# Opening loads reordered and tied to TensorE's progress, and one scores visit moved

## The chip, the cores and the metric

The kernel runs on one core of one Trainium2 chip. The metric is the device time of one execution in microseconds (us). Loads from HBM are issued on two hardware queues here: most by the SyncE sequencer (SP), a few at the very start by ScalarE (ACT).

## The reference

```
scores = scale * q @ k.T          # 8 batches, 8 heads, 576 positions, head 64
scores = where(mask, scores, -1e9)  # heads 0-3: the last 32 positions; heads 4-7: 32 of the last 128, every 4th
attn   = exp(scores - max); attn = attn / (sum(attn) + 1e-9)
x      = (attn @ v) laid out as (4608 tokens, 512)
h      = x @ w_in                 # 512 -> 2048
g      = max(h, 0) + log1p(exp(-abs(h)))
out    = g @ w_out                # 2048 -> 512
```

## The kernel before

The 4608 tokens are cut into nine chunks of 512. Attention goes by groups: chunk c and pair of heads, `groups[4c + pr]`. The steps of a group have one letter each. S is the scores (`score`, 64 small matmuls into `s_ps`; the first two chunks add the mask with two more matmuls of a bf16 identity, held in the tile `opened`), M the maximum on VectorE (DVE), E eight exponentials on ACT (line 421), Z the divisor, Pv the division on DVE, T four transposes on TensorE (`t_ps`, line 450), C or Cv the copy back (`pt`), V the product with v (64 small matmuls into `a_ps`), Xh and Xl the split of the result into a high and a low part (`xh`, `xl`). The feed-forward part runs in slots: one slot is one chunk and one of 16 slices ff of the hidden width. `H` is a quarter of the first product (three matmuls 128x512 into `h_ps`), A its three activations on ACT, G the softplus on DVE, Gs and Gl the split into `gh` and `gl`, `O` a quarter of the second product (`o_ps`).

The weights arrive as 64-bit floats. `fetch` loads raw piece r_n as two loads of 256 KB; `decode_step` turns it into two fp32 parts by D0 (ACT) , D1 to D4 (DVE), D5 (ACT) and Dl (DVE). D0_ff_i begins piece (ff, i), i = 0 for w_in and 1 for w_out; r0 is (0, 0), r1 (1, 0), r2 (0, 1), r3 (2, 0).

The first 45 us and some more are written out by hand: the string `OPENING` (line 73) lists the steps, and a loop after line 762 issues them in that order. Each engine works through its own instructions in the order of the string, so a token's place decides only what stands ahead of it on its engine. `F` is a run of filler matmuls on a zeroed tile (`unread`), `r k q v m` are loads. Group loads: k 272 or 320 KB, q 256 KB, v twice 256 KB, the mask of chunk 1 (m1) 128 KB; m0 is the identity and the mask of chunk 0, 160 KB into `opened`. The keys of groups 0 to 2 and m0 go out on ACT's queue, all other loads on SP's. `load_dma` (line 137) lets each of the first THIN = 64 loads on SP wait until the load DEPTH = 8 places earlier has landed. TensorE needs q and k of a group for S, v for V.

After the opening the attention of the later chunks is put between the slots by due times. `attend(n, when, lag)` places, for the groups n and n+1, the scores at slot time `when` (`scores`), the row maxima, exponentials and divisions after it, and the product with v at `when + lag`. A cost given with each step also tells the planner in `tick` when DVE has room for the remaining decoding and for the sums of weights that the later chunks need (`early`). From chunk 2 on the first product is done by sums and differences of blocks (`h_x`, `h_y`).

Of the kernel before, what the change touches and what calls it, by code (L numbers as in the profile page):

```python
# [40 lines left out]
NPR = H // 2  # L41
# [4 lines left out]
FIRST = 2  # L46
# [3 lines left out]
EARLY = 5  # L50
NEG = -1.0e9
DEPTH = 8
THIN = 64
LAG = 2
EXP_AND_LN = [t.name for t in act_sets.SETS].index("natural_log_exp_and_others")

# [14 lines left out]


OPENING = """
F1 r0 k0 m0 q0 r1 k1 q1 r2 k2 q2 k3 q3 v0 q4 k4 m1 v1 r3 k5 v2 q5 v3 r4 r5 D0_0_0 v4 F6 D1_0_0 S0
D2_0_0 D3_0_0 D4_0_0 F1 D5_0_0 D0_1_0 M0 E0 Dl0_0 r6 r7 D1_1_0 D2_1_0 D3_1_0 S1 v5 M1 Z0 D0_0_1 Pv0
D1_0_1 S2 D2_0_1 M2 D3_0_1 E1 Z1 T0 S3 D4_0_1 Pv1 C0 V0 E2 M3 T1 Cv1 Xh0 Xl0 F3 S4 D4_1_0 E3 Z2 M4
q7 Pv2 k7 V1 H0_0 Xh1 D0_2_0 Xl1 D1_2_0 r8 r9 T2 E4 k6 Cv2 Z3 H0_1 D2_2_0 D5_1_0 Pv3 q6 r10 D3_2_0
V2 Dl1_0 S5 M5 D5_0_1 Xh2 Xl2 T3 Dl0_1 H1_0 H1_1 Z4 C3 E5 Pv4 D4_2_0 V3 Z5 Xh3 D0_3_0 D5_2_0 Xl3 Pv5
T4 H0_2 D1_3_0 D2_3_0 H0_3 D3_3_0 C4 V4 A0 H1_2 H1_3 D0_1_1 Xh4 Dl2_0 G0 D1_1_1 H2_0 H2_1 Xl4 H2_2
T5 D2_1_1 D3_1_1 Gs0 Gl0 D0_4_0 A1 D4_3_0 D4_1_1 C5 H2_3 D1_4_0 D2_4_0 G1 O0_0 O0_1 O0_2 O0_3 V5  # L80
D5_3_0 Dl3_0 H3_0 H3_1 H3_2 D5_1_1 D3_4_0 Gs1 H3_3 D4_4_0 Dl1_1 Gl1 O1_0 v7 D0_2_1 D1_2_1 D2_2_1 Xh5
D3_2_1 Xl5 A2 G2 D5_4_0 D4_2_1 r11 Dl4_0 v6 r12 r13 A3 G3 Gs2 D5_2_1 Gl2 D0_5_0 O1_1 r14 Dl2_1 r15
D0_3_1 O1_2 S7 M7 H4_0 H4_1 O1_3 r16 H4_2 D1_5_0 E7 D2_5_0 D3_5_0 O2_0 O2_1 r17 O2_2 H4_3 D4_5_0
D5_5_0 D1_3_1 r18 r19 r20 S6 r21 O2_3 D2_3_1 D3_3_1 r22 Dl5_0 H5_0 H5_1 H5_2 Gs3 A4 M6 Gl3 G4 E6
D4_3_1 Z7 H5_3 Gh4 Pv7 D5_3_1 Dl3_1 H6_0 H6_1 T7 D0_4_1 r23 C7 D1_4_1 Z6 O3_0 O3_1 D2_4_1 A5 Pv6
D3_4_1 D4_4_1 G5 V7 Xh7 Xl7 O3_2 D5_4_1 Dl4_1 Gl4 O3_3 H7_0 T6 D0_5_1 r24 r25 Cv6 H7_1 O4_0 D1_5_1
V6 D2_5_1 D3_5_1 D0_6_0 r26 O4_1 O4_2 O4_3 Gs5 Gl5 Xh6 Xl6 H6_2 H6_3 D1_6_0 D0_6_1 H7_2 D4_5_1
D1_6_1 D2_6_1 D5_5_1 Dl5_1 r27 r28 r29 D3_6_1 A6 D4_6_1 G6 Gh6 Gl6 H7_3 A7 G7 O5_0 O5_1 O5_2 O5_3
H8_0 H9_0 H8_1 r30 r31 K0 D5_6_1 K1 D2_6_0 D0_9_0 D1_9_0 Gs7 H8_2 H8_3 A8 Dl6_1 O6_0 Gl7 H9_1 D3_6_0
D4_6_0 H9_2 H9_3 K2 K3 D5_6_0 D2_9_0 O6_1 D3_9_0 D4_9_0 D5_9_0 G8 Dl9_0 Dl6_0 O6_2 O6_3 Gh8 O7_0 Gl8  # L90
O7_1 O7_2 A9 O7_3 G9 Gh9 Gl9
"""


# [1 line left out]
def tile_windowed_attention_softplus_ffn(  # L96
# [11 lines left out]
    nc = tc.nc  # L108
# [11 lines left out]
    slots, at = [], {0: 0, 1: 0}  # L120
# [11 lines left out]

        tc.keep_in_program_order(ins)

    under_way = []

    def load_dma(engine=None, **kw):
        ins = tc.keep_in_program_order((engine or nc.sync).dma_start(**kw))
        if engine is None and len(under_way) < THIN:
            if len(under_way) >= DEPTH:  # L140
                tc.add_manual_dep(
                    ins.ins,
                    under_way[-DEPTH].ins.name,
                    mybir.DependencyInfo(mybir.DependencyClass.Sync, mybir.DependencyReason.DATA),
                    reason="at most so many of the first loads under way",
                )
            under_way.append(ins)

    def load_halves(out, in_):

        n = out.shape[1] // 2
        for half in (slice(0, n), slice(n, 2 * n)):
            load_dma(out=out[:, half], in_=in_[:, half])

    def fetch(upto):
        for _, ff, i in needed[len(raws) : upto]:
            raw = const.tile([P, DM], mybir.dt.int64, name="raw", tag=f"w{ff}_{i}")
            load_halves(raw, w[ff, :, i * DM : (i + 1) * DM])
            raws[ff, i] = raw
# [40 lines left out]
            wt[ff, i] = parts  # L200

    def matmul(**kw):
        tc.keep_in_program_order(nc.tensor.matmul(**kw))  # L203

    def bank(name, tag):
        return psum.tile([P, CH], F32, name=name, tag=tag, bufs=2 if tag == "h" else 1)
# [31 lines left out]
    def load_mask(c):  # L238
        if c == 0:
            load_dma(nc.scalar, out=consts, in_=cst[0])  # L240
            nc.gpsimd.tensor_copy(out=ident, in_=identb)
            masks[0] = consts[:, P:]
            return
        masks[c] = wk.tile([P, 2 * SW], BF16, name="mask", bufs=2)
        load_dma(out=masks[c], in_=cst[c, :, P:] if c < FIRST else msk[c])
# [75 lines left out]
    class Group:  # L321
# [33 lines left out]
        def score(self, both=None):  # L355

            self.base = 0 if both is None else self.pr % 2 * SW
            self.banks, self.scored = both or two_banks(
                "s_ps", "hh" if self.own and self.pr % 2 else None
            )  # L360
            for t in range(NS):
                for g in range(NG):
                    for r in range(2):
                        rows = slice(r * D, (r + 1) * D)
                        q0, k0 = first_of(self.dil, t, g, self.c >= FIRST)
                        matmul(
                            out=self.banks[r][
                                g * BLK : (g + 1) * BLK,
                                self.base + t * WKEYS : self.base + (t + 1) * WKEYS,
                            ],  # L370
                            lhsT=self.q[rows, q0 : q0 + BLK],
                            rhs=self.k[rows, k0 : k0 + WKEYS],
                            start=not self.masked or t == 0,
                            stop=not self.masked,
                        )
# [214 lines left out]
    groups = [Group(c, pr) for c in range(NCH) for pr in range(NPR)]  # L590
# [38 lines left out]
    def at(when, part, *what, cost=0.0):  # L629
        heapq.heappush(events, (when, next(serial), cost, part, what))  # L630
# [126 lines left out]
    def fillers(n):  # L757
# [3 lines left out]

    parts = {
        "F": fillers,
        "k": lambda g: groups[g].load_k(nc.scalar if g < 3 else None),
        "q": lambda g: groups[g].load_q(),
        "v": lambda g: groups[g].load_v(),
        "m": load_mask,
        "r": lambda n: fetch(n + 1),
        "S": lambda g: groups[g].score(),
        "M": lambda g: groups[g].maximum(),  # L770
# [142 lines left out]
    def attend(n, when, lag, wait=0.0):  # L913

        at(when, scores, n, cost=-1.45)
        for e in range(2):
            g, then = groups[n + e], when + e
            late = 0 if e else wait
            at(then + 0.12 + late, g.maximum, cost=1.34)
            at(then + 0.37 + late, g.exponentials)  # L920
            at(then + 1.0, g.divisor, cost=0.36)
            at(then + 1.0, g.divide)
            at(then + 1.37, turn, n + e, cost=0.65)
            at(then + 1.5, send, n + e)
            at(then + 2.2, bring, n + e)
        at(when + 2.8, load_v, n + 1)
        at(when + 3.45, load_queries, n + 2)
        at(when + lag, values, n, cost=-1.45)
        for e in range(2):
            at(when + lag + 0.25 + 0.25 * e, groups[n + e].turn_rows, cost=0.65)  # L930
        at(when + lag + 0.7, groups[n].send_x)
        back = 3.0 if n == (FIRST + 1) * NPR else 1.25
        at(when + lag + back, groups[n].bring_x)
        at(when + lag + 0.01, load_keys, n + 2)
        at(when + lag + back + 0.05, load_v, n + 2)
# [24 lines left out]
    for ff in range(NFF):  # L960
        at(18 + 0.55 * ff if ff < 4 else 22.4 + 0.4 * (ff - 4), keep_w_out, ff)
    for j in range(2):
        attend(FIRST * NPR + 2 * j, 10.2 + 7.5 * j, 4.125)
    attend((FIRST + 1) * NPR, 26.7, 4.6, 0.25)
    at(26.2, ob_tiles, 0, True)
    for n in range(4):
# [81 lines left out]
    behind = 0.0  # L1048
# [122 lines left out]
    for n, (c, p) in enumerate((c, p) for c in range(FIRST, NCH) for p in range(NPAIR)):  # L1171
        u = 2 * n
        for k, (x, weights, b, first, to, temp) in enumerate(steps):
# [20 lines left out]
    for half in range(2):  # L1194
        ob = const.tile([P, NKT, HALF], F32, name="pt", tag=("s", "v")[half])
        for m in range(NKT):
# [7 lines left out]
            if half and m > 1:  # L1204
                engine = nc.sync if m % 2 else nc.scalar
# [126 lines left out]
```

## Time and profile before

| | |
|---|---|
| median of three timed runs | 867.06 us (866.37 to 868.7) |
| the profiled execution, device time | 867.87 us |
| its span, first to last instruction | 866.0 us |
| TensorE matmul busy | 847.8 us, 98% of the span, 9143 matmuls |
| VectorE, ScalarE busy | 618.3 us, 533.4 us |
| mean granted TensorE clock | 0.996 of full |
| largest shares of the chain that ended last | o_ps 44%, h_x 19%, h_y 14%, h_ps 9% |

The span is read from the first instruction to the last; the device time is 1.87 us longer. TensorE executes its instructions in order, so each idle stretch of it is a row of the timeline with the time and, in brackets, the idle time before it and what ended it. "issue" there means that the engine waited for nothing that the profile shows. The DMA queues are listed by kind: q1 and q10 are the loads and stores that SP and ACT issue, q8 and q14 are of the kind "instruction".

### The profile page before, as it was taken

The page shows a single profiled execution, that of the slowest core. Times are in us where ns is not written, and L with a number is a line of the kernel's source. Part 1 is how long each engine was busy: PE and PEld are TensorE (multiplying, and loading weights), DVE is VectorE, ACT ScalarE, POOL GpSimd, SP SyncE. Part 2 cuts the span into 40 slices and gives each one's busy share as a digit, 9 for nine tenths or more (in the row PEclk, how much of TensorE's full clock was granted, in tenths as well). Part 3 has the DMA queues.
Part 4 walks back from the last instruction along what each step waited for, and adds up shares of the span by engine and source line. Part 5 has one row for each costly group of instructions (what it writes and reads, how often), then busy time and mean ns, then how long its engine had stood idle before and what let it go on. Part 6 is the DMA issues. An engine that isn't in the chain of part 4 may idle for free.

```text
span 866.0 us, 22770 instructions
## 1 busy us (share of the span) xinstructions
PE 847.8 (98%) x9143; PEld 735.5 (85%) x9143; DVE 618.3 (71%) x1260; ACT 533.4 (62%) x1327; POOL 31.4 (4%) x34
## 2 busy tenths in 40 slices
PE   6799999999999999999999999999999999999998
PEld 4478888888888988888888989898889898899997
DVE  5698898898888887576856777576748675665554
ACT  5587778767565767466564665565736564465443
POOL 0000000101000000000000000000000000000000
PEclk9899999999999999999999999999999999999999
DMA  9849445684666475657575656556664754424223
GB/s 329 310 135 383 175 128 172 200 307 167 192 221 207 151 247 179 211 181 231 197 229 158 210 196 218 196 181 216 210 215 154 231 195 157 146 98 146 98 107 113
DMA packets 107305, 168.81 MB, mean 195 GB/s; under 512 B 11072, under 2 KB 41920, under 8 KB 107200
## 3 DMA queue, kind: packets, MB, share of 16 engines
q1 hardware_dynamic: 106480, 166.18, 58.0%
q8 instruction: 72, 1.18, 0.6%
q10 hardware_dynamic: 720, 1.18, 0.4%
q14 instruction: 33, 0.27, 0.1%
HBM read 132.71 MB, written 34.60 MB: 193 GB/s over the span
## 4 chain that ended last, share of the span: by engine, by line
PE 93%; DVE 3%; ACT 2%; issue 1%; DMA 1%; SPq 0%; ACTq 0%
PE o_ps L203 44%; PE h_x L203 19%; PE h_y L203 14%; PE h_ps L203 9%; PE s_ps L203 3%; PE a_ps L203 3%; ACT s L421 1%; DMA raw<-w 1%; PE t_ps L450 0%; DVE e L673 0%; DVE t L843 0%; ACT a L171 0%; DVE b L823 0%; DVE ob L746 0%; DVE gl L691 0%
## 5 line engine op out<-in xcount | busy, mean ns | idle before, releaser
L203 PE MATMUL o_ps<-gh,t 128*128 128x512 f32 (+1 forms) x904 | 341.3, 391 | 0.0
L203 PEld LDWEIGHTS o_ps<-gh,t 128*128 128x128 f32 x904 | 169.8, 188 | 21.6
L666 ACT ACTIVATE e<-hs 128x512 f32<-128x512 f32 x112 | 70.0, 625 | 186.7 <-DVE hs L1100 186.6
L203 PE MATMUL o_ps<-gl,t 128*128 128x512 f32 (+1 forms) x452 | 178.4, 395 | 0.0
L685 ACT CAST gh<-e 128x512 fp32r<-128x512 f32 x140 | 86.4, 617 | 64.5 <-DVE e L673 60.0
L691 DVE TENSOR_TENSOR gl<-e,gh 128x512 fp32r<-128x512 f32 x144 | 103.1, 716 | 5.5 <-ACT gh L685 4.7
L203 PEld LDWEIGHTS h_x<-a,parts 128*128 128x128 f32 x672 | 94.7, 189 | 10.2 <-DVE temps L1098 0.7
L203 PEld LDWEIGHTS h_y<-s,t 128*128 128x128 f32 x672 | 94.4, 188 | 10.0 <-DVE temps L1100 0.2
L203 PE MATMUL h_x<-a,parts 128*128 128x256 f32 x672 | 98.6, 282 | 0.2 <-DVE temps L1098 0.2
L203 PE MATMUL h_y<-s,t 128*128 128x256 f32 x672 | 98.8, 282 | 0.0
L668 ACT ACTIVATE e<-e 128x512 f32<-128x512 f32 x144 | 91.2, 633 | 4.6
L667 ACT ACTIVATE e<-e 128x512 f32<-128x512 f32 x144 | 91.1, 633 | 4.6
L203 PEld LDWEIGHTS o_ps<-gl,t 128*128 128x128 f32 x452 | 86.4, 191 | 3.0 <-DVE gl L691 0.4
L203 PE MATMUL h_ps<-xh,parts 128*128 128x512 f32 x256 | 88.0, 399 | 0.0
L203 PE MATMUL o_ps<-gh,parts 128*128 128x512 f32 x256 | 87.0, 393 | 0.0
L1100 DVE TENSOR_TENSOR hs<-h_x,temps 128x256 f32<-128x256 f32 x112 | 47.3, 422 | 52.5 <-PE h_x L203 51.9
L421 ACT ACTIVATE s<-s,nm 128x64 f32<-128x64 f32 x224 | 74.8, 335 | 5.6 <-DVE nm L413 5.5
L673 DVE SCALAR_TENSOR_TENSOR e<-hs,e 128x512 f32<-128x512 f32 x112 | 76.2, 681 | 1.8 <-ACT e L668 1.8
L1100 DVE TENSOR_TENSOR temps<-h_y,temps 128x256 f32<-128x256 f32 x112 | 47.2, 421 | 41.4 <-PE h_y L203 40.8
L1098 DVE COPY temps<-h_x 128x256 f32<-128x256 f32 x56 | 23.6, 422 | 56.4 <-PE h_x L203 56.3
L203 PEld LDWEIGHTS h_ps<-xh,parts 128*128 128x128 f32 x256 | 48.6, 190 | 10.6 <-DVE e L673 0.5
L203 PEld LDWEIGHTS o_ps<-gh,parts 128*128 128x128 f32 x256 | 48.1, 188 | 9.9
(82 smaller groups left out, 1189.6 us busy)
## 6 DMA issues: line engine op xcount, KB each, us to landing
t<-w_out SPq DMA_DIRECT2D x224, 256.0 KB, 3.2
raw<-w SPq DMA_DIRECT2D x64, 256.0 KB, 5.6
v<-vp SPq DMA_DIRECT2D x28, 512.0 KB, 4.6
q<-qp SPq DMA_DIRECT2D x36, 256.0 KB, 4.9
w_out<-parts SPq DMA_DIRECT2D x16, 512.0 KB, 6.8
out_t<-ob SPq DMA_DIRECT2D x32, 256.0 KB, 2.9
turned<-sq SPq DMA_DIRECT2D x112, 64.0 KB, 2.6
pt<-turned SPq DMA_DIRECT2D x28, 256.0 KB, 2.8
```

Source lines behind the costliest of these rows:

```text
L203: tc.keep_in_program_order(nc.tensor.matmul(**kw))
L421: pin(nc.scalar.activation(out=self.blocks[:, t], in_=src, func=AF.Exp, bias=self.nm[:, t : t + 1], scale=1.0 / 8.0 if self.masked else 1. ...
L666: pin(nc.scalar.activation(out=e, in_=tiles[i], func=AF.Abs))
L667: pin(nc.scalar.activation(out=e, in_=e, func=AF.Exp, scale=-1.0))
L668: pin(nc.scalar.activation(out=e, in_=e, func=AF.Ln, bias=1.0))
L673: pin(nc.vector.scalar_tensor_tensor(out=e, in0=tiles.pop(i), scalar=0.0, in1=e, op0=ALU.max, op1=ALU.add))
L685: pin((copy or nc.scalar.copy)(out=gh, in_=ready[i]))
L691: pin(nc.vector.tensor_tensor(out=gl, in0=e, in1=gh.bitcast(F32), op=ALU.subtract))
L1098: pin(nc.vector.tensor_copy(out=dst, in_=src))
L1100: pin(nc.vector.tensor_tensor(out=dst, in0=src, in1=temps[:, temp], op=ALU.add))
```

## The change

The string `OPENING` keeps the sequence of every engine but SP and ACT's load queue, and its loads stand in another order and mostly later. A new token W remembers the newest matmul issued through `matmul` (not the transposes of T); the next load on SP that follows in the string gets a wait for that matmul. As SP issues in order, all loads behind it are held too. THIN goes from 64 to 128. The keys of group 2 move from ACT's queue to SP's. The second visit of `attend` (groups 10 and 11) has its scores at 16.575 instead of 17.7 slots; its lag goes from 4.125 to 5.25, so its product with v stays at 21.825.

```diff
-THIN = 64
+THIN = 128
 OPENING = """
-F1 r0 k0 m0 q0 r1 k1 q1 r2 k2 q2 k3 q3 v0 q4 k4 m1 v1 r3 k5 v2 q5 v3 r4 r5 D0_0_0 v4 F6 D1_0_0 S0
+m0 q0 r0 k1 k0 F1 D0_0_0 F6 r1 D1_0_0 S0 q1 D2_0_0 k2 D3_0_0 r2 D4_0_0 F1 D5_0_0 D0_1_0 M0 E0 W1 q2
...
     def load_dma(engine=None, **kw):
         ins = tc.keep_in_program_order((engine or nc.sync).dma_start(**kw))
+        if engine is None and gate:
+            depends(ins, gate.pop(), "loads behind what TensorE does")
...
     def matmul(**kw):
-        tc.keep_in_program_order(nc.tensor.matmul(**kw))
+        newest[:] = [tc.keep_in_program_order(nc.tensor.matmul(**kw))]
...
-        "k": lambda g: groups[g].load_k(nc.scalar if g < 3 else None),
+        "k": lambda g: groups[g].load_k(nc.scalar if g < 2 else None),
...
+        "W": lambda _: gate.append(newest[0]),
...
-        attend(FIRST * NPR + 2 * j, 10.2 + 7.5 * j, 4.125)
+        attend(FIRST * NPR + 2 * j, (10.2, 16.575)[j], (4.125, 5.25)[j])
```

The gated loads and their gates, in SP's order: q2 and q3 behind the filler after S0; k4 (then m1) behind S2; q4 (then v1, r3) behind S3; q5 (then v2, k5, r4, v3) behind S4; q7 (then r5, v4, r6) behind V2; k7 (then r7, r8, v6, v5, r9, k6, r10, r11) behind V3; v7 (then q6, r12, r13 to r16) behind O1_1; r17 to r31 behind three later steps.

First place: SP at the start of the program, before. A DMAHW name is the lane of an earlier load whose landing is awaited.

```order
L138 DMA raw<-w 128x256 x2
L138 DMA q<-qp 128x512
L138 DMA raw<-w 128x256
L138 DMA raw<-w 128x256 [waits DMAHW0_50]
L138 DMA q<-qp 128x512 [waits DMAHW1_50]
L138 DMA raw<-w 128x256 [waits DMAHW2_50]
L138 DMA raw<-w 128x256 [waits DMAHW3_50]
L138 DMA q<-qp 128x512 [waits DMAHW4_50]
L138 DMA k<-kdl 128x640 [waits DMAHW5_50]
L138 DMA q<-qp 128x512 [waits DMAHW6_50]
L138 DMA v<-vp 128x512 [waits DMAHW7_50]
L138 DMA v<-vp 128x512 [waits DMAHW0_50]
```

The same place of SP in the change, from the first load to the first of k4; PE is the wait that W adds.

```order
L146 DMA q<-qp 128x512
L146 DMA raw<-w 128x256 x4
L146 DMA q<-qp 128x512 [waits DMAHW0_50]
L146 DMA k<-kdl 128x640 [waits DMAHW1_50]
L146 DMA raw<-w 128x256 [waits DMAHW2_50]
L146 DMA raw<-w 128x256 [waits DMAHW3_50]
L146 DMA q<-qp 128x512 [waits DMAHW4_50,PE_50]
L146 DMA q<-qp 128x512 [waits DMAHW5_50]
L146 DMA k<-kdl 128x640 [waits DMAHW6_50]
L146 DMA v<-vp 128x512 [waits DMAHW7_50]
L146 DMA v<-vp 128x512 [waits DMAHW0_50]
L146 DMA k<-kpl 128x544 [waits DMAHW1_50,PE_50]
```

q0 stands ahead of r0 and r1 now, the third q (q2) waits for TensorE, and what follows v0 begins with a gated k4.

Second place: ACT at the start of the program, before.

```order
L138 DMA k<-kpl 128x544
L138 DMA opened<-cst 128x640
L138 DMA k<-kpl 128x544
L138 DMA k<-kdl 128x640
L171 ACTIVATE a<-raw 128x512
```

ACT in the change, to the decoding of r1.

```order
L146 DMA opened<-cst 128x640
L146 DMA k<-kpl 128x544 x2
L176 ACTIVATE a<-raw 128x512
L199 CAST parts<-a 128x512
L176 ACTIVATE a<-raw 128x512
```

m0 is first, k1 and k0 follow, and k2 is no longer here; the work behind the loads keeps its sequence.

Third place: TensorE (PE) in slots 16 and 17, in the change, where the scores of groups 10 and 11 stand now.

```order
L208 MATMUL s_ps<-k,q 32x64 x64
L208 MATMUL o_ps_1458<-gh,parts 128x512
L208 MATMUL o_ps_1458<-gl,parts 128x512
L208 MATMUL o_ps_1458<-gh,parts 128x512
L208 MATMUL o_ps_1469<-gh,parts 128x512
L208 MATMUL o_ps_1469<-gl,parts 128x512
L208 MATMUL o_ps_1469<-gh,parts 128x512
```

PE before, one slot later, where the same scores stood.

```order
L203 MATMUL o_ps_1458<-gh,parts 128x512
L203 MATMUL s_ps<-k,q 32x64 x64
L203 MATMUL o_ps_1469<-gh,parts 128x512
L203 MATMUL o_ps_1469<-gl,parts 128x512
L203 MATMUL o_ps_1469<-gh,parts 128x512
```

The visit stands 27 matmuls of 128x512 earlier; nothing else moves on TensorE. On DVE and ACT the row maxima and exponentials of this visit move up by about as much, and some decoding steps and sums of weights move down behind them.

## Rows read from the trace of the kernel before

**Rows 1.** The page's part 1: busy us, share of the span and instructions of each engine.
```profile
PE 847.8 (98%) x9143; PEld 735.5 (85%) x9143; DVE 618.3 (71%) x1260; ACT 533.4 (62%) x1327; POOL 31.4 (4%) x34
```

**Rows 2.** TensorE's waits from 45 us on: engine, line, releaser: us, times, longest.
```profile
PE h_x L203 <- DVE hs L1098: 0.6, 1, 0.6
PE h_x L203 <- DVE temps L1098: 0.2, 1, 0.2
```

**Rows 3.** Timeline of PE, 0 to 44 us: start, us, what [idle before <- releaser].
```profile
8.13 1.17 PE L203 MATMUL s_ps<-k,q 64*32 64x64 f32 x64 [3.43 <-DMA q<-qp]
...
13.40 1.18 PE L203 MATMUL s_ps<-k,q 64*32 64x64 f32 x64 [0.78 <-ACT s L421]
...
17.21 1.10 PE L203 MATMUL s_ps<-k,q 64*32 64x64 f32 x55 [0.40 <-issue]
...
18.79 1.94 PE L203 MATMUL a_ps<-pt,v 64*64 64x32 f32 x64
...
24.09 1.12 PE L203 MATMUL a_ps<-pt,v 64*64 64x32 f32 x60
27.29 0.30 PE L203 MATMUL a_ps<-pt,v 64*64 64x32 f32 x4 [2.07 <-issue]
...
31.00 0.73 PE L203 MATMUL s_ps<-k,q 64*32 64x64 f32 x48 [0.17 <-ACT s L421]
35.75 0.47 PE L203 MATMUL s_ps<-k,q 64*32 64x64 f32 x16 [4.02 <-issue]
...
43.50 1.14 PE L203 MATMUL a_ps<-pt,v 64*64 64x32 f32 x64 [0.31 <-ACT pt L488]
```

**Rows 4.** Windows from one stop of PE to the next: busy (xcount), clock, DMA, GB/s.
```profile
16.90:27.20 10.30, 8.00 (x254) 5.76 (x253) 6.57 (x18) 5.68 (x35) 0.00 (x0) 1.00 1.01 353
27.20:35.70 8.50, 4.18 (x126) 3.22 (x127) 3.91 (x9) 4.88 (x22) 0.00 (x0) 0.85 1.00 334
```

**Rows 5.** The page's part 3, one queue of kind instruction: packets, MB, share.
```profile
q8 instruction: 72, 1.18, 0.6%
```

**Rows 6.** DMA from 24.8 to 33.3 us: packets, queue, issues with us to landing.
```profile
DMA packets 1462, 2.66 MB, mean 313 GB/s; under 512 B 164, under 2 KB 164, under 8 KB 1462
...
q1 hardware_dynamic: 1462, 2.66, 97.3%
...
raw<-w SPq DMA_DIRECT2D x7, 256.0 KB, 6.3
```

**Rows 7.** DMA from 33.3 to 33.6 us: the instruction queue's packet.
```profile
q8 instruction: 1, 0.02, 19.8%
```

**Rows 8.** DMA from 43.8 to 45 us: all packets, and their queue.
```profile
DMA packets 1, 0.02 MB, mean 14 GB/s; under 512 B 0, under 2 KB 0, under 8 KB 0
...
q8 instruction: 1, 0.02, 6.2%
```

**Rows 9.** Timeline of SP's queue around 25 us: start, us, loads issued.
```profile
24.77 3.03 SPq L138 DMA_DIRECT2D raw<-w  x4
```

**Rows 10.** DMA from 53.3 to 53.7 us: a load issued into empty queues.
```profile
v<-vp SPq DMA_DIRECT2D x1, 256.0 KB, 3.1
```

**Rows 11.** Timeline of ACT, 6 to 43 us: start, us, what [idle before <- releaser].
```profile
6.64 0.66 ACT L171 ACTIVATE a<-raw 128x512 f32<-128x512 f32 x1 [4.63 <-DMA raw<-w]
...
10.87 0.31 ACT L421 ACTIVATE s<-s_ps,nm 128x64 f32<-128x64 f32 x1
...
15.90 0.35 ACT L421 ACTIVATE s<-s_ps,nm 128x64 f32<-128x64 f32 x1
...
28.48 0.31 ACT L421 ACTIVATE s<-s_ps,nm 128x64 f32<-128x64 f32 x1
...
41.24 0.65 ACT L584 CAST xh<-a_ps 128x256 fp32r<-128x256 f32 x2 [0.63 <-PE a_ps L203]
```

**Rows 12.** Windows around PE's longest stop: busy of PE, PEld, DVE, ACT, POOL, then clock.
```profile
32.00:36.00 4.00, 0.25 (x16) 0.23 (x15) 0.18 (x1) 0.52 (x2) 0.00 (x0) 0.64 1.02 370
36.00:40.00 4.00, 4.00 (x28) 2.85 (x12) 3.10 (x9) 2.35 (x14) 0.00 (x0) 0.50 1.04 396
```

**Rows 13.** Windows around the old place of the moved scores visit (same columns).
```profile
135.00:145.00 10.00, 10.00 (x166) 8.21 (x165) 9.20 (x18) 8.13 (x15) 0.00 (x0) 1.00 0.25 95
```

More of the change, by code (lines that the diff above doesn't have):

```diff
@@ L73 @@
 OPENING = """
-F1 r0 k0 m0 q0 r1 k1 q1 r2 k2 q2 k3 q3 v0 q4 k4 m1 v1 r3 k5 v2 q5 v3 r4 r5 D0_0_0 v4 F6 D1_0_0 S0
[L75 to L90, printed above, removed]
@@ L91 @@
-O7_1 O7_2 A9 O7_3 G9 Gh9 Gl9
+m0 q0 r0 k1 k0 F1 D0_0_0 F6 r1 D1_0_0 S0 q1 D2_0_0 k2 D3_0_0 r2 D4_0_0 F1 D5_0_0 D0_1_0 M0 E0 W1 q2
+Dl0_0 D1_1_0 D2_1_0 W1 D3_1_0 S1 q3 M1 Z0 D0_0_1 Pv0 D1_0_1 S2 D2_0_1 M2 D3_0_1 E1 k3 Z1 v0 T0 W1 k4
+S3 m1 W1 q4 D4_0_1 v1 r3 Pv1 C0 V0 E2 M3 T1 Cv1 Xh0 Xl0 F3 S4 D4_1_0 E3 Z2 M4 Pv2 W1 W1 V1 H0_0 Xh1
+D0_2_0 Xl1 D1_2_0 T2 E4 q5 Cv2 Z3 v2 k5 H0_1 D2_2_0 r4 D5_1_0 v3 Pv3 D3_2_0 V2 Dl1_0 W1 S5 M5 D5_0_1
+Xh2 Xl2 T3 Dl0_1 H1_0 H1_1 Z4 C3 E5 Pv4 D4_2_0 q7 V3 Z5 Xh3 r5 D0_3_0 v4 r6 D5_2_0 W1 Xl3 Pv5 T4
@@ new lines @@
+H0_2 D1_3_0 k7 D2_3_0 H0_3 D3_3_0 C4 V4 A0 H1_2 H1_3 D0_1_1 Xh4 Dl2_0 r7 r8 v6 G0 D1_1_1 H2_0 H2_1
+Xl4 H2_2 T5 D2_1_1 D3_1_1 Gs0 Gl0 D0_4_0 A1 D4_3_0 D4_1_1 v5 C5 H2_3 r9 D1_4_0 D2_4_0 G1 O0_0 O0_1
+O0_2 O0_3 V5 D5_3_0 Dl3_0 H3_0 H3_1 H3_2 D5_1_1 D3_4_0 Gs1 H3_3 D4_4_0 Dl1_1 Gl1 k6 O1_0 D0_2_1
+D1_2_1 D2_2_1 Xh5 D3_2_1 Xl5 A2 G2 D5_4_0 D4_2_1 Dl4_0 A3 r10 G3 Gs2 D5_2_1 Gl2 D0_5_0 r11 O1_1
+Dl2_1 D0_3_1 W1 O1_2 S7 v7 M7 H4_0 H4_1 O1_3 H4_2 D1_5_0 E7 D2_5_0 D3_5_0 O2_0 O2_1 O2_2 q6 H4_3
+D4_5_0 D5_5_0 D1_3_1 S6 O2_3 D2_3_1 D3_3_1 r12 Dl5_0 H5_0 H5_1 H5_2 Gs3 A4 M6 Gl3 G4 E6 D4_3_1 Z7
@@ new lines @@
+H5_3 Gh4 Pv7 D5_3_1 Dl3_1 H6_0 H6_1 T7 D0_4_1 C7 D1_4_1 r13 Z6 O3_0 O3_1 D2_4_1 A5 Pv6 D3_4_1 D4_4_1
+G5 V7 Xh7 r14 r15 r16 Xl7 O3_2 W1 D5_4_1 r17 r18 r19 r20 Dl4_1 Gl4 O3_3 H7_0 T6 D0_5_1 W1 Cv6 H7_1
+r21 O4_0 D1_5_1 V6 D2_5_1 D3_5_1 D0_6_0 O4_1 O4_2 O4_3 Gs5 r22 r23 r24 Gl5 Xh6 Xl6 H6_2 H6_3 D1_6_0
+r25 r26 r27 r28 r29 D0_6_1 H7_2 D4_5_1 D1_6_1 r30 D2_6_1 D5_5_1 Dl5_1 D3_6_1 W1 A6 D4_6_1 G6 Gh6 Gl6
+H7_3 A7 G7 O5_0 O5_1 O5_2 O5_3 r31 H8_0 W1 H9_0 H8_1 K0 D5_6_1 K1 D2_6_0 D0_9_0 D1_9_0 Gs7 H8_2 H8_3
@@ L92 @@
+A8 W1 Dl6_1 O6_0 Gl7 H9_1 D3_6_0 D4_6_0 H9_2 H9_3 K2 K3 D5_6_0 D2_9_0 O6_1 D3_9_0 D4_9_0 D5_9_0 G8
+Dl9_0 Dl6_0 O6_2 O6_3 Gh8 O7_0 Gl8 O7_1 O7_2 A9 O7_3 G9 Gh9 Gl9
 """
@@ L133, in pin, with depends @@
         tc.keep_in_program_order(ins)
-    under_way = []
+    under_way, gate, newest = [], [], []
+    def depends(ins, on, reason):
+        tc.add_manual_dep(
+            ins.ins,
+            on.ins.name,
+            mybir.DependencyInfo(mybir.DependencyClass.Sync, mybir.DependencyReason.DATA),
+            reason=reason,
+        )
     def load_dma(engine=None, **kw):
         ins = tc.keep_in_program_order((engine or nc.sync).dma_start(**kw))
+        if engine is None and gate:
+            depends(ins, gate.pop(), "loads behind what TensorE does")
         if engine is None and len(under_way) < THIN:
             if len(under_way) >= DEPTH:
[L141 to L146, printed above, removed]
+                depends(ins, under_way[-DEPTH], "at most so many of the first loads under way")
             under_way.append(ins)
```

## The prediction

> **What bounds the kernel now.** I read the page's busy times first: TensorE is busy for 98% of the span [rows 1], so only time that it loses can be won. Its waits from 45 us to the end add up to 0.8 us [rows 2]; the rest of its idle time lies in the first 45 us, which the change rewrites. The timeline of that stretch [rows 3] shows three kinds of loss. S0 waits for q0 until 8.13. S2 waits until 13.40 for ACT, whose exponentials E0 must free the bank. And three times TensorE waits for "issue", that is for nothing that the profile shows: 0.40 us in S3, 2.07 in V1, 4.02 in S5.
>
> What are these three? Between the first and the second stop lie 254 matmuls, between the second and the third 126 [rows 4]. Each matmul has a weight load, so that is about 508 and 252 instructions. The page counts 9143 matmuls and 9143 weight loads [rows 1] and 72 packets on the instruction queue q8 [rows 5]: 18286 / 72 = 254 per packet. So TensorE stops where a block of its own instructions ends and the next is not there. The DMA rows agree: from 24.8 to 33.3 us all 1462 packets belong to q1, none to q8 [rows 6]; TensorE stops at 31.73 (31.00 + 0.73); the q8 packet begins between 33.3 and 33.6 [rows 7]; TensorE goes on at 35.75, some 2.4 us after it.
>
> Why is it late? I read it as queued behind loads. SP issued four raw loads from 24.77 over 3.03 us [rows 9], and loads of that stretch take 6.3 us to land [rows 6]. TensorE entered the last block before the stop at 27.29, and 27.29 + 6.3 = 33.6, just where the packet is. With no load under way, a single packet of q8 passes between 43.8 and 45 us [rows 8], and TensorE doesn't stop for it. [...]
>
> **The change part by part.** THIN, 64 to 128: nothing. In the order, loads beyond the eighth already wait for a lane that an earlier load holds, and the added wait names a load of that kind.
>
> The moved visit: nothing on TensorE's sum, which keeps its 64 matmuls per group. It stands 27 matmuls earlier; TensorE is busy for the whole of its window, and DVE for 9.20 of 10 us [rows 13]. What DVE does later for it is decoding and sums of weights, and TensorE shows no wait for these in that stretch [rows 2]. Bounds: a gain of the 0.8 us of waits there are, a loss of as much. On SP the loads and sends of the visit move up past some stores of w_out, on POOL its divisions move up; neither is waited for there. I take 0.
>
> The first loads: m0, k1 and k0 on ACT's queue, q0, r0 and r1 on SP's. S0 needs q0, k0 and m0. Up to now r0 led: its second half was down when ACT began decoding at 6.64 [rows 11], and S0 got q0 at 8.13. Now q0, m0 and k1 go ahead of r0 and k0 beside it: 256 + 160 + 272 + 512 + 272 = 1472 KB until r0 and k0 are complete. That is what r0, k0, m0, q0 and k1 were, and of those q0 ended the wait at 8.13. So S0 stays near 8.1, and r0 comes at about 8.1 instead of 6.64, **1.5 us later** (bounds 0 and 2). Decoding of r0 stands ahead of M0 on DVE and ahead of E0 on ACT, so E0 moves from 10.87 [rows 11] to 12.4, S2 from 13.40 to 14.9, and the last exponential of E1 from 15.90 + 0.35 = 16.25 to 17.75. S3 needs the bank that E1 frees; its last 55 matmuls now run from 17.21 because of the stop [rows 3]. Without the stop they would run from 17.75: **+0.55** for V0 (18.79 to 19.35). k2, moved to SP behind r1 and q1, is in about 512 + 256 + 320 KB later, at 353 GB/s [rows 4] near 11.2, well before S2. Most of the late start is thus covered by the 0.40 us stop and the time that S3 already lost.
>
> The gates: what is queued when TensorE enters a block. At 353 GB/s [rows 4] a 256 KB load takes 0.74 us of queue. For the stop in V1 the block before begins at the fillers, about 22.6 in the new count. Ahead of its refill stand q4, v1 and r3: five loads, 3.7 us, released by S3's end at 19.5. For the stop in S5 the block before begins at V1's end; the gate on S4 (24.9) lets q5, v2 and k5 out by then, four loads, about 3 us, where eight were under way. A load into empty queues lands in 3.1 us [rows 10], one behind others in 6.3 [rows 6]. So the refills still wait, but behind a queue that was empty shortly before and has been draining since. The bounds of each stop are 0 and what it is today, 2.07 and 4.02. Counting from when data begin to move, about 1 us after issue, I get queue ends near 24 and 28.5, and with 2.4 us to restart, 26.4 and 30.9, against 25.8 and 30.6 wanted. I take **0.7 us left of each**: -1.35 and -3.3.
>
> [...] I take 0.63, and 0.12 on the end of S5: **-0.75**, between 0 and -2.0.
>
> What the gates delay: q4 is wanted at S4, about 23.6. Released at 19.5, it lands at 22.6 by [rows 10]. v2's second half, the third load behind S4, is wanted near 28.5 and lands at 24.9 + 3.1 + 2 x 0.74 = 29.5 by the same count, less if the 3.1 holds the wait of its own refill. That is level, so I add nothing. v6 waits for V4 and holds v5 back, with 7 us until V5. Later pieces have many slots.
>
> Sum: +0.55 - 1.35 - 3.3 - 0.75 = -4.85 us. The profiled execution took 867.87 us, so 863.0. The median of the runs shown is 0.81 lower: 862.2.
>
> **The rivals.** *The refills still queue.* Each gate lets out a burst that stands ahead of the next refill. For it: loads are issued 0.4 us apart once free, and both refills come 2 to 3 us after a gate. Then V1's stop stays at 2.07, S5's goes to 1.9 by the smaller burst, and the clock holds: 0.55 - 2.1 - 0.75 = -2.3, 864.8.
>
> *Everything is covered.* Both stops go, and r0 comes early enough that S3 follows E1 without loss: -2.07 - 4.02 - 0.75 - 0.4 = -7.25, 859.8.
>
> *The stops have nothing to do with the loads.* The packets of q8 would come when they come; only the late r0 remains, and the stops of 2.07 and 4.02 stay: 867.06 + 0.55 = 867.6. Against it stand the 6.3 us that fit and the unharmed refill at 44 us. [...]
>
> *Slower: TensorE starves and stays at the low clock.* The place is S4. If q4 lands more than 4.1 us after its gate, S4 waits; at 6.3 it begins at 25.8, 2.2 us late. The gap could keep the lower level through V2: V0 took 1.94 us there and V4 1.14 at the higher, so V1 and V2 lose 1.6, S4 and S5 0.6, transposes and six h matmuls about 2.0. v2, behind the next gate, would be late by 2.2 again. With the 0.55 that is 0.55 + 2.2 + 2.2 + 4.2 = 9.15, against 6.1 for the stops, which slower work would hide, and nothing from the clock: +3.05, 870.1.
>
> **How the numbers follow.** A measurement of this kernel tells about 0.3%, 2.6 us, from no change. Forecast 0.60; refills still queue 0.14; all covered 0.13; stops unrelated 0.07; starved 0.06. Faster by over 2.6 us: 0.60 + 0.13 + 0.04 of the second case = 0.77. Within: 0.10 + 0.06 = 0.16. Slower: 0.07, the starved case and a little of the unrelated one. The range 859.3 to 865.9 takes in the second and the third case and leaves out the last two.
>
> **What would show it.** Right: "issue" before V1 and S5 under 1 us each; granted clock 1.00 from 24 to 40 us; ACT's first decoding near 8.1; V4 near 38.7 instead of 43.5; no new wait after 45 us. Wrong: a wait for DMA at S4, V2 or S5, an "issue" stop of 2 us or more, or a clock that falls again.

## The result and the profile after

The change made the kernel **slower: 872.17 us** (median of five executions, 870.92 to 875.06) against 867.06 us (865.92 to 868.89), a ratio of 1.0056 with the interval [1.0039, 1.0073]. Forecast were 862.2 us and a range of 859.3 to 865.9. The profiled execution has a span of 872.7 us, 6.7 us more than before; its device time, 875.06 us, is the longest of the five, so it shows somewhat more than the 5.1 us between the medians. The page's part 1, after (engine, busy us, share of the span, instructions), answers to [rows 1]: TensorE is busy 5.2 us longer with the same matmuls (one record fewer), and idle 1.5 us longer (19.7 against 18.2).

```profile
PE 853.0 (98%) x9142; PEld 740.0 (85%) x9143; DVE 619.3 (71%) x1260; ACT 533.7 (61%) x1327; POOL 31.4 (4%) x34
```

The prediction spoke of the first 45 us. The timeline of TensorE there, after (start, us, what, and in brackets the idle time before it and what ended it), against [rows 3]:

```profile
8.45 1.17 PE L208 MATMUL s_ps<-k,q 64*32 64x64 f32 x64 [3.76 <-DMA k<-kpl]
...
14.58 1.18 PE L208 MATMUL s_ps<-k,q 64*32 64x64 f32 x64 [2.33 <-ACT s L426]
...
19.14 1.94 PE L208 MATMUL a_ps<-pt,v 64*64 64x32 f32 x64
...
22.34 1.06 PE L208 MATMUL unread<-opened 128*128 128x512 bf16 x2 [0.22 <-DMA q<-qp]
23.33 1.05 PE L208 MATMUL s_ps<-k,q 64*32 64x64 f32 x64
24.31 0.39 PE L208 MATMUL s_ps<-mask,opened 128*128 128x256 bf16 x2
24.63 1.12 PE L208 MATMUL a_ps<-pt,v 64*64 64x32 f32 x60
28.04 0.42 PE L208 MATMUL a_ps<-pt,v 64*64 64x32 f32 x4 [2.29 <-issue]
...
35.63 0.47 PE L208 MATMUL s_ps<-k,q 64*32 64x64 f32 x16 [0.69 <-issue]
...
43.79 1.14 PE L208 MATMUL a_ps<-pt,v 64*64 64x32 f32 x64 [0.31 <-ACT pt L493]
```

S2 and V0 begin where the prediction put them (14.9 and 19.35 were forecast). S3's stop is gone. But V1's stop is 2.29 us, not 0.7, and V4 begins at 43.79, not 38.7: 0.29 us later than before. S5's stop has the forecast length, 0.69 us, and yet nothing is won there: S5 goes on at 35.63, against 35.75 before. It is TensorE that comes to the stop later, at 33.97 + 0.97 = 34.94 instead of 31.73. The q8 packet after which it goes on comes between 33.3 and 33.6 us, as before [rows 7]:

```profile
q8 instruction: 1, 0.02, 18.3%
```

The windows say why TensorE came to S5 so late (length, busy of PE, PEld, DVE, ACT and POOL with counts, granted clock, DMA share, GB/s):

```profile
24.00:28.00 4.00, 1.75 (x94) 1.34 (x78) 2.25 (x7) 0.51 (x3) 0.00 (x0) 0.90 0.69 217
28.00:32.00 4.00, 3.96 (x14) 2.85 (x14) 1.88 (x6) 3.49 (x19) 0.00 (x0) 0.50 0.92 310
32.00:36.00 4.00, 3.31 (x129) 2.76 (x128) 2.04 (x4) 1.51 (x4) 0.00 (x0) 0.50 0.37 117
36.00:40.00 4.00, 4.00 (x22) 2.88 (x16) 3.22 (x9) 2.47 (x15) 0.00 (x0) 0.50 0.95 310
```

The granted clock is 0.90 in the window that holds V1's stop, 0.50 in the next three and 0.89 in the one after them. Before, it was 0.50 in one such window and 0.64 in the one ahead of it [rows 12].

The loss itself lies elsewhere, in a stretch that the prediction does not reach. The first line of TensorE's waits over the whole execution, after (us, times, longest):

```profile
PE s_ps L208 <- DMA k<-kpl: 7.8, 3, 3.8
```

Of the three waits for keys, one is S0's 3.76 us. The timeline around 100 us shows the other two, in the scores of groups 8 and 9, the first of chunk 2:

```profile
98.79 0.39 PE L208 MATMUL h_ps<-xh,parts 128*128 128x512 f32 x1
102.64 1.17 PE L208 MATMUL s_ps<-k,q 64*32 64x64 f32 x64 [3.47 <-DMA k<-kpl]
104.36 1.17 PE L208 MATMUL s_ps<-k,q 64*32 64x64 f32 x64 [0.55 <-DMA k<-kpl]
105.46 0.79 PE L208 MATMUL h_ps<-xh,parts 128*128 128x512 f32 x1
...
129.84 1.51 PE L208 MATMUL a_ps<-v,pt 64*32 64x64 f32 x128
```

And before:

```profile
98.89 1.51 PE L203 MATMUL s_ps<-k,q 64*32 64x64 f32 x128
100.33 0.50 PE L203 MATMUL h_ps<-xh,parts 128*128 128x512 f32 x1
...
123.00 1.51 PE L203 MATMUL a_ps<-v,pt 64*32 64x64 f32 x128
```

TensorE enters this stretch 0.22 us behind its time before (98.79 against 98.57 for the same matmul). At 105.46 it is 5.1 us behind, at 129.84 it is 6.84 us behind, which is the whole difference of the spans. 3.47 + 0.55 = 4.0 us are the waits. The other 2.6 us I put down to the clock: it was granted at 0.79 and 0.50 in these windows, at 1.00 in both before, and the scores of the two groups take 1.17 us each, where both together took 1.51.

```profile
100.00:104.00 4.00, 1.17 (x64) 0.96 (x64) 1.99 (x4) 1.18 (x2) 0.00 (x0) 0.79 1.06 397
104.00:108.00 4.00, 3.63 (x70) 3.01 (x71) 2.39 (x4) 0.00 (x0) 0.00 (x0) 0.50 0.77 290
```

Why were the keys late? What SP's queue itself waited for between 40 and 110 us, after:

```profile
SPq L146 <- PE o_ps L208: 15.2, 2, 9.4
SPq L146 <- DMA raw<-w: 11.6, 31, 1.2
```

The two waits for o_ps are new. They are the gates behind O1_1 and O3_2; the second holds SP for 9.4 us and ends at about 74.8, when r17 goes out. The transfers from there to 97.2 us (queue: packets, MB, share of the 16 engines; then issues with KB and us to landing):

```profile
q1 hardware_dynamic: 3720, 6.79, 89.9%
...
raw<-w SPq DMA_DIRECT2D x30, 256.0 KB, 5.9
k<-kpl SPq DMA_DIRECT2D x1, 272.0 KB, 5.4
```

First come 30 raw loads, with which the DMA engines are busy for 90% of the time, and behind them, at the first K of the string, the queries and keys of groups 8 and 9. The keys of group 8 on SP, after and before:

```profile
97.11 0.33 SPq L146 DMA_DIRECT2D k<-kpl  x1
```

```profile
87.26 0.33 SPq L138 DMA_DIRECT2D k<-kpl  x1
```

They go out 9.85 us later and take 5.4 us to land: 97.11 + 5.4 = 102.5, and the scores that were due at 98.9 begin at 102.64. That is theory A: the late gates make the keys late through the order of the queue. The first experiments put it against two rivals: the loss comes from the opening's low clock, or from the moved visit.

### The profile page after: what moved, and what is told of

Its sections match the earlier page's. It is cut to its first block, busy times and chain, and to the rows that moved or that the text cites. A ratio compares the mean times of both kernels' runs of the same rounds, so it can differ in the third digit from the quotient of the medians.

```text
span 872.7 us, 22779 instructions
## 1 busy us (share of the span) xinstructions
PE 853.0 (98%) x9142; PEld 740.0 (85%) x9143; DVE 619.3 (71%) x1260; ACT 533.7 (61%) x1327; POOL 31.4 (4%) x34
## 4 chain that ended last, share of the span: by engine, by line
PE 91%; DMA 3%; DVE 3%; ACT 1%; issue 1%; SPq 0%; ACTq 0%
PE o_ps L208 43%; PE h_x L208 18%; PE h_y L208 14%; PE h_ps L208 8%; PE s_ps L208 4%; PE a_ps L208 3%; DMA raw<-w 2%; DMA k<-kpl 1%; ACT s L426 1%; PE t_ps L455 1%; DVE e L678 0%; DVE t L849 0%; DVE b L829 0%; SPq L146 0%; DVE ob L751 0%
## 5 line engine op out<-in xcount | busy, mean ns | idle before, releaser
L208 PE MATMUL h_ps<-xh,parts 128*128 128x512 f32 x256 | 90.0, 407 | 0.0
L426 ACT ACTIVATE s<-s,nm 128x64 f32<-128x64 f32 x224 | 74.8, 335 | 5.5 <-DVE nm L418 5.3
```

The lines of the kernel that those rows point to most:

```text
L208: newest[:] = [tc.keep_in_program_order(nc.tensor.matmul(**kw))]
L426: pin(nc.scalar.activation(out=self.blocks[:, t], in_=src, func=AF.Exp, bias=self.nm[:, t : t + 1], scale=1.0 / 8.0 if self.masked else 1. ...
```

## The experiments

Each kernel was timed beside the kernel before on the same chip, whose medians lay between 867.5 and 867.8 us in these comparisons.

**The late gates away.** The changed kernel without the six gates from O1_1 on:

```diff
-D0_3_1 W1 O1_2
+D0_3_1 O1_2
-O3_2 W1 D5_4_1
+O3_2 D5_4_1
...
-D0_5_1 W1 Cv6
+D0_5_1 Cv6
-D3_6_1 W1 A6
+D3_6_1 A6
-H8_0 W1 H9_0
+H8_0 H9_0
-A8 W1 Dl6_1
+A8 Dl6_1
```

> The change without its six gates from O1_1 on; the earlier gates and the order of the loads stay. Theory A (the whole loss is SP standing still: 5.8 us before O1_1 and 9.4 us before O3_2, so that k8 lands at 102.5 when TensorE wants it at 98.9): no wait for k<-kpl at 99 us, the granted clock stays at 1.00 from 96 to 108 us, V4 still near 43.8, and the time is that of the kernel before plus 0.3: 866.5 to 868.0 us. Rival (the loads are late by their place in the order, or the opening costs time later): the wait at 99 us stays, 871 to 873 us.

Measured: 866.46 us, ratio 0.9989 [0.9977, 1.0002]. The scores of groups 8 and 9 run without a wait, as TensorE's timeline shows, and the clock is granted at 1.00 from 100 to 108 us:

```profile
97.06 1.51 PE L208 MATMUL s_ps<-k,q 64*32 64x64 f32 x128
```

So the late gates are the loss, all of it. The opening with its new order is left in, and with it the kernel is not measurably faster than before. V4 begins at 41.74 in this execution, not near 43.8 as expected, though the opening is that of the changed kernel.

**One late gate alone.** The kernel before, with r17 to r23 moved from their places behind a gate on O3_2, and W's few lines (of r18 to r23 the removal is left out):

```diff
-O2_0 O2_1 r17 O2_2
+O2_0 O2_1 O2_2
...
-O3_2 D5_4_1
+O3_2 W1 D5_4_1 r17 r18 r19 r20 r21 r22 r23
```

> The kernel before with one gate alone: r17 to r23 stand behind O3_2 and wait for it, all else as before. Theory A: SP stands still until about 75 us, k8 lands near 102 us, TensorE waits about 3.5 us for it near 99 us and loses 2 to 3 us more at the lower clock: 872 to 873.5 us. Rival (a late piece of weights is made up for later): 866.5 to 868 us.

Measured: 872.81 us, ratio 1.0063 [1.0041, 1.0085]. That is the whole loss from one gate, with the old opening. Its timeline of TensorE, with the opening's stops first and the late keys below:

```profile
28.46 0.42 PE L210 MATMUL a_ps<-pt,v 64*64 64x32 f32 x4 [2.87 <-issue]
...
35.77 0.47 PE L210 MATMUL s_ps<-k,q 64*32 64x64 f32 x16 [0.41 <-issue]
...
42.78 1.14 PE L210 MATMUL a_ps<-pt,v 64*64 64x32 f32 x64
...
100.66 0.85 PE L210 MATMUL s_ps<-k,q 64*32 64x64 f32 x64 [2.27 <-DMA k<-kpl]
102.38 1.05 PE L210 MATMUL s_ps<-k,q 64*32 64x64 f32 x64 [0.88 <-DMA k<-kpl]
```

The keys cost 2.27 + 0.88 = 3.2 us, and the clock falls to 0.75 in the window from 104 to 108 us.

**All gates, but the keys ahead.** This asks whether the place in the queue does it, or the late raw pieces themselves. The changed kernel, with q, k, the mask and v of chunk 2's first groups loaded ahead of r25 instead of behind r31:

```diff
-r25 r26 r27 r28 r29 D0_6_1
+L0 r25 r26 r27 r28 r29 D0_6_1
...
     def keep(m):
-        if m == 0:
-            load(2 * NPR)
-            load(2 * NPR + 1)
-            load_v(2 * NPR)
         kept_part(m, *keeping.pop(m))
+    def ahead(_):
+        load(2 * NPR)
+        load(2 * NPR + 1)
+        load_v(2 * NPR)
+    parts["L"] = ahead
```

> The changed kernel with all its holds, but the first loads of chunk 2 (q and k of groups 8 and 9, the mask, v of group 8) stand ahead of r25 to r31 in SP's queue instead of behind them. Theory A (the loss is the place of these loads behind thirty raw loads that the hold on O3_2 makes late): they are issued some 14 raw loads of 0.67 us, 9 to 10 us, earlier than at 96.5, near 87, and land near 92.5; S8 at about 99 us waits for nothing, the granted clock stays at full level from 100 to 108 us, and the time falls from 872.2 to 866 to 867.5. The raw pieces r25 to r31 land 4 to 5 us later than in the changed kernel; if that matters, a wait for parts (the last pieces of w_out) shows up between 100 and 125 us. Rival 1: the late raw pieces are the real loss and S8's wait only its first sign: the time stays at 870 to 873 with a new wait for decoded weights or a DVE that falls behind. Rival 2: the loss sits in the opening (half clock from 27 to 41 us): the time stays at 871 to 872 though S8 waits for nothing.

Measured: 867.7 us, ratio 0.9995 [0.998, 1.001]. The keys go out at 84.21 on SP, TensorE waits for nothing near 100 us, and among its waits there is none for what r25 to r31 become:

```profile
84.21 0.33 SPq L146 DMA_DIRECT2D k<-kpl  x1
```

```profile
96.13 1.65 PE L208 MATMUL s_ps<-k,q 64*32 64x64 f32 x128
```

The keys go out some 3 us earlier than expected, and the median is 0.2 us above what theory A gave. With every gate in place and only six loads moved, the loss is gone. Theory A is shown from three sides; both rivals in that run fall.

**The moved visit alone.** The kernel before with the second visit of attend at 16.575:

```diff
-        attend(FIRST * NPR + 2 * j, 10.2 + 7.5 * j, 4.125)
+        attend(FIRST * NPR + 2 * j, (10.2, 16.575)[j], (4.125, 5.25)[j])
```

> The kernel before with nothing but the scores visit of groups 10 and 11 at 16.575 slots. Theory A: no price, 866.5 to 867.6 us, TensorE without a wait from 45 to 200 us. Rival (the moved visit takes part in the loss through VectorE's order): 868 us or more, with a wait of TensorE between 130 and 250 us.

Measured: 866.88 us, ratio 0.9993 [0.9981, 1.0004]. The moved visit costs nothing and gives nothing. This run taught more than that. Its opening is instruction for instruction that of the kernel before, yet its stops are other ones:

```profile
27.81 0.30 PE L203 MATMUL a_ps<-pt,v 64*64 64x32 f32 x4 [1.91 <-issue]
...
34.35 0.35 PE L203 MATMUL s_ps<-k,q 64*32 64x64 f32 x16 [0.96 <-issue]
...
40.69 1.14 PE L203 MATMUL a_ps<-pt,v 64*64 64x32 f32 x64
```

S5's 4.02 us [rows 3] is 0.96 here, and 0.41 in the kernel with one late gate alone (fence above), which has the old opening too. The length alone misleads, though. S5 goes on at 35.75 us before, at 35.77 with one late gate alone and at 34.35 here. Where the stop is short, V1's stop and the lower clock behind it (0.57 from 28 to 32 us here, 0.50 from 28 to 36 with one late gate alone) had already made TensorE late.

**The opening's own question.** Do refills of TensorE's instructions (so I read the packets on q8, one to 254 instructions by [rows 1] and [rows 5]) queue behind loads, as I had read it? Theory B: yes, and V1's stop stayed because the gate on S3 lets out a burst just ahead of the refill. In the first test, r3 goes out earlier, so that the burst is smaller (late gates away here and in the next two):

```diff
-v0 T0 W1 k4
+v0 r3 T0 W1 k4
...
-D4_0_1 v1 r3 Pv1
+D4_0_1 v1 Pv1
```

> As the run without late gates, and r3 goes right behind v0, ahead of the gate of k4, into the stretch in which the queue is empty; so three loads (q4, v1) instead of five stand ahead of the refill that V1 waits for. Theory B (the opening gained nothing because the stop of 2.29 us in V1 brought the clock down from 27.6 to 40.4 us): the stop in V1 falls below 1.2 us, the granted clock stays at 1.00 from 24 to 36 us, V4 begins near 40, and the time is 862 to 864.5 us. Rival (the refill isn't behind the loads, or the clock falls for the earlier gap before S2): the stop stays at 2 us or the clock falls all the same, 866.5 to 868 us.

Measured: 867.38 us, ratio 0.9997 [0.9984, 1.0009]. V1's stop became 1.41 us, S5's 2.52:

```profile
26.15 0.30 PE L208 MATMUL a_ps<-pt,v 64*64 64x32 f32 x4 [1.41 <-issue]
...
34.85 0.47 PE L208 MATMUL s_ps<-k,q 64*32 64x64 f32 x16 [2.52 <-issue]
```

And the clock fell all the same, between the two stops; the window of 4 us around V2:

```profile
28.00:32.00 4.00, 3.46 (x108) 2.63 (x109) 3.07 (x7) 3.49 (x17) 0.00 (x0) 0.70 0.92 309
```

With the smaller burst V1's stop is shorter and S5's longer than with the late gates away (2.70 and 0.90); the time is that of the rival, and by the stops alone this neither shows theory B nor refutes it.

In the second test the gates stand right behind the entry of each block, so that, if theory B holds, the refill finds little ahead of it:

```diff
-v0 T0 W1 k4
-S3 m1 W1 q4 D4_0_1 v1 r3 Pv1
+v0 r3 T0 W1 k4 q4
+m1 S3 W1 D4_0_1 v1 Pv1
...
-F3 S4 D4_1_0 E3 Z2 M4 Pv2 W1 W1 V1 H0_0
+F3 W1 q5 v2 k5 S4 D4_1_0 E3 Z2 M4 Pv2 V1 W1 v3 r4 H0_0
...
-V2 Dl1_0 W1 S5 M5
+V2 Dl1_0 S5 W1 M5
```

> No late gates; the early gates are moved to just behind the places where TensorE enters a new block of instructions: r3 behind v0, q4 with k4 behind S2, v1 behind S3, q5, v2, k5 behind the third filler F3, v3, r4 behind V1, q7, r5, v4, r6 behind S5. Theory B (a refill waits for the loads issued before TensorE enters the block before): each refill finds one or two loads ahead of it at most, the stops for issue in V1 and S5 are under 0.6 us each, the clock doesn't fall between 24 and 36 us, V4 begins at 38 to 40 us, and the time is 862 to 865 us. Rival 1 (the refills are late whatever the queue holds): stops of 1 to 4 us in V1 or S5 as in the other executions, 866 to 868 us. Rival 2 (the stops go but the clock falls for other gaps, or ACT's chain bounds the opening): stops under 0.6 us, V4 later than 41 us, 865.5 to 867.5 us.

Measured: 866.52 us (863.19 to 872.94, 12 executions), ratio 0.9989 [0.997, 1.0008]. The median misses the 862 to 865 us of theory B. In the profiled execution V1 and S5 no longer stop for issue, and V4 begins 5.1 us earlier than before, where theory B put it:

```profile
24.97 1.57 PE L208 MATMUL a_ps<-pt,v 64*64 64x32 f32 x64
...
30.23 0.86 PE L208 MATMUL s_ps<-k,q 64*32 64x64 f32 x64 [0.16 <-ACT s L426]
...
34.97 0.66 PE L455 MATMUL t_ps<-opened,s 128*128 128x128 f32 x4 [0.67 <-ACT s L426]
...
38.40 1.13 PE L208 MATMUL a_ps<-pt,v 64*64 64x32 f32 x64 [1.37 <-ACT pt L493]
```

The refill packet itself tells more. V1's stop comes 2 + 64 + 2 + 60 = 128 matmuls, 256 instructions with their weight loads, after the fillers at 22.34 (timeline above), so by this count the block before it begins there; TensorE's sequence is the same in both kernels. In the changed kernel SP issued five loads from 19.24 on (q4, v1, r3), and the packet came between 25.7 and 26.0 us, over 3 us after the fillers; the DMA rows of that stretch have it:

```profile
q8 instruction: 1, 0.02, 18.3%
```

In this experiment the fillers begin at 22.33, only v1's two loads go out in that time (the next, q5, at 23.41), and the packet came between 22.8 and 23.0, about half a microsecond after:

```profile
q8 instruction: 1, 0.02, 27.4%
```

The other executions fall in line by the time at which TensorE goes on. With the same five loads ahead, V1 goes on 5.7 us after the fillers in the changed kernel (28.04 against 22.34), 6.4 with the late gates away (27.02 against 20.64) and 5.8 with the keys ahead (26.89 against 21.07); with three loads ahead (r3 earlier) it goes on 4.8 us after them (26.15 against 21.38). So the packet came later with five loads ahead than with two, and V1's stop ended later, counted from the fillers, with five than with three. That the refill queues behind the loads is my reading of it; where on its way the refill was held, no run shows.

The third test puts the old head back, r0 first, on top of the gates at block entries:

```diff
-m0 q0 r0 k1 k0 F1 D0_0_0 F6
+r0 k0 m0 q0 k1 F1 D0_0_0 F6
```

> As the run before it, with the first loads in the old order (r0, q0, r1 on SP, k0, m0, k1 on ACT). Theory C (q0 ahead of r0 costs the opening 1.2 us on ACT's chain, E0 at 12.06 instead of 10.87, as the changed kernel's trace shows): E0 begins near 10.9, S2 near 13.4, V4 about 1.2 us earlier than in the run before it, and the time is 0.5 to 1.2 us lower. Rival (what is won at the head is lost again at the next refill or load): V4 and the time within 0.5 us of the run before it.

Measured: 866.75 us, ratio 0.9995 [0.9979, 1.0011]. What r0 wins at the head is lost at the next load: S2 waits for q2, and S5 stops again, with the clock at 0.50 from 32 to 36 us. V4 begins at 40.66, 2.3 us later than in the run before it, which is neither theory C nor its rival.

```profile
14.73 1.17 PE L208 MATMUL s_ps<-k,q 64*32 64x64 f32 x64 [2.86 <-DMA q<-qp]
...
32.56 0.47 PE L208 MATMUL s_ps<-k,q 64*32 64x64 f32 x16 [2.31 <-issue]
```

The stop in S5 also limits what the gates' place can do. V1 again has no stop for issue: its 64 matmuls stand in one row, from 24.45. S5 stops for 2.31 us here, and in the run before it ran its 64 matmuls in one row from 30.23. The gates stand in the same places in both, so the place alone does not settle it, and no run shows what does.

**What the openings are worth.** One number of the timeline sums an opening up: the start of V4. Against the span of the same execution:

| profiled execution | V4 begins | span | span less V4 |
|---|---|---|---|
| before | 43.50 | 866.0 | 822.5 |
| moved visit alone | 40.69 | 863.6 | 822.9 |
| keys ahead | 40.71 | 863.5 | 822.8 |
| late gates away | 41.74 | 863.7 | 822.0 |
| r3 earlier | 43.28 | 865.9 | 822.6 |
| gates at block entries | 38.40 | 862.8 | 824.4 |
| old head on top | 40.66 | 864.2 | 823.5 |
| one late gate alone | 42.78 | 870.0 | 827.2 |
| after | 43.79 | 872.7 | 828.9 |

Five kernels without the loss agree within 0.9 us in the last column: what an opening gains to V4, the end gains. The last two rows carry the late keys, 4 to 7 us more. And the V4 of one and the same opening goes from 40.69 to 43.50 (first, second and eighth row), which is as much as most of these edits move it. The changed opening spreads as far: 43.79, 41.74 and 40.71 (after, late gates away, keys ahead). By this number it can't be told from the old one (43.50, 40.69, 42.78). The gates at block entries win 5.1 us to V4, but the end shows 1.9 us less of it. V4 itself waits 1.37 us for ACT's copy, and ACT had waited for a raw piece ahead of it:

```profile
36.69 0.66 ACT L176 ACTIVATE a<-raw 128x512 f32<-128x512 f32 x1 [1.24 <-DMA raw<-w]
```

That wait lies ahead of V4 and is in its start already. Behind V4, from 39.5 to 42.9, the 128x512 matmuls begin 0.43 us apart, against 0.23 from 45.74 on; by that I put the price of these 3.4 us at about half, 1.6, and so most of the 1.9. TensorE had waited 0.67 and 1.37 us for ACT ahead of that; whether this brought the clock down, no run shows. The granted clock is 0.62 in the window there:

```profile
40.00:44.00 4.00, 4.00 (x13) 3.16 (x12) 3.76 (x7) 2.47 (x6) 0.00 (x0) 0.62 1.01 313
```

Over 12 executions it is about 1 us ahead of the kernel before by the median, and the interval of its ratio reaches past 1. No version clearly beats both kernels.

## Why the prediction was wrong

**The step that failed** is the sentence on what the gates delay: "Later pieces have many slots." I counted nothing for the gates from O1_1 on, because the decoding of the last raw pieces has time. It has: with the keys ahead, r25 to r31 went out behind them (from 87.51 on), and TensorE never waited for them. But SP issues in the order of the string, and I did not follow its queue past r31 to the next load that somebody needs at once. The gate on O3_2 holds SP for 9.4 us, the queue does not make that up (the DMA engines are busy for 90% of the time with the 30 raw loads behind it), and so q and k of group 8 go out 10 us late. The price: 4.0 us of waits and, by my estimate, some 2.6 us of lower clock in the profiled execution, 5.1 us between the medians. No rival of mine held this; the slower one put its starvation at S4, where q4 came in time but for 0.22 us.

**The rest of the sum failed too.** Without the late gates the change gave 0.9989 [0.9977, 1.0002], not 4.85 us less.

**-3.3 for S5's stop: wrong, and its length came out by luck.** The stop shrank to 0.69, but it ended at 35.63 instead of 35.75. The end of the queue was put near 28.5, with four loads ahead of the refill and data that begin to move about 1 us after issue (before, a load of v was issued at 53.39 into empty queues and its first data moved at 54.3); the packet came after 33.3. V1's stop put off V1's end to past 28.04, and by then SP had issued six loads of the gate on S4 and went on with the next two:

```profile
28.01 0.90 SPq L146 DMA_DIRECT2D v<-vp  x2
```

Nor was 4.02 us a fixed price. The same opening showed 0.96 and 0.41 in two others, with V4 at 40.69 and 42.78 instead of 43.50. I took a stall of one execution for a property of the kernel. No run shows the 0.75 us that the sum takes off beside it: in the change the clock was granted at 0.50 in three windows of 4 us, against one before, and V4 began 0.29 us later.

**-1.35 for V1's stop: wrong.** It stayed at 2.29, above the upper bound of 2.07. The end of the queue was put near 24; the refill packet came after 25.7. The rival in which the refills still queue had this part right, but not its clock.

**The clock: wrong.** It was to be 1.00 from 24 to 40 us. Before, it was 1.00 from 24 to 32 us, around the stop of 2.07 us. In the change it fell in the stop of 2.29 us, from 1.00 in the window from 26.7 to 27.0 us to 0.50 in that from 27.5 to 28.0, and was 0.50 up to 40 us; V2 took 1.93 us there, against 1.14 for V4 (0.89 from 40 to 44 us, 1.00 from 44 to 48). With V1's stop this made TensorE 3.2 us late at S5, where it would have waited for the packet anyway.

**What was right.** The late r0: ACT's first decoding at 7.85 (about 8.1 forecast), S2 at 14.58, V0 at 19.14, each within 0.35 us. THIN and the moved visit at 0: the visit alone gives 0.9993 [0.9981, 1.0004]; THIN was not run alone, but it is 128 in the kernel without late gates too, which loses nothing. The reading of the stops, as far as the packets show it: one packet to 254 instructions, and V1's packet 3.4 to 3.7 us after the fillers with five loads ahead and 0.5 to 0.7 us after them with only two, issued well before. The rival in which the stops have nothing to do with loads doesn't fit these two packets.

**What stays open:** why the clock falls behind some stops and not behind others of about the same length, why the stops of one opening differ between executions, and why S5 stopped once and ran through once with the same gates. Whether gates at block entries gain 1 us or nothing was not settled by 12 executions.

## What to carry to other kernels

SP issued its loads in the order of the string, and with the hold on O3_2 ahead of 30 raw loads the keys of group 8, behind these, went out 9.85 us later. So follow the queue behind a hold to the first load whose consumer is due, and put that load ahead of the hold. Before a stall is entered as a term, look for it in a second execution of the same instructions, and read when it ends as well as how long it lasts; here a 4.02 us stop was 0.41 in another execution, and the two ended 0.02 us apart. Where TensorE stops for issue at a block's end while loads are queued, look at what is queued when the block before it is entered: here, letting the burst out just after the entry rather than just before took V1's stop away in two of two executions, S5's in one of two, and the time did not move beyond the noise.

## What was not expected of the hardware

The stops for issue differ in executions of the same opening: S5's were 4.02, 0.96 and 0.41 us, V1's 2.07, 1.91 and 2.87. And the granted clock does not follow the length of a stop alone. It held at 1.00 over the 2.07 us stop of the kernel before [rows 4], where V2 then, from 29.70, took 1.14 us. With the same instructions (the moved visit alone) it was down to 0.57 in the window from 28 to 32 us, behind a stop of 1.91 us. And it was down to 0.70 in that window of the kernel with r3 earlier, behind a stop of 1.41 us; there TensorE had waited 0.54 us for q4 and then run S4 and 60 of V1's matmuls before it stopped.

Ahead of about 23 us the rows of the granted clock do not always fit the durations. V0 took 1.94 us before [rows 3], as long as V2 in the change at 0.50 (1.93), where the window that holds it gives 1.00 [rows 4]; in the change V0, at 19.14, took 1.94 us as well, and the clock there is 1.00 from 16 to 24 us. So the prediction's reading of V0 as work at the lower level rests on its duration and not on the row of the clock.
